# Turning x of two batches by DMA transposes instead of on TensorE, in an attention and mixture-of-experts kernel

## The chip, the core and the metric

The kernel runs on one core of a Trainium2 chip. The core has five engines with their own instruction streams: TensorE (PE, matmuls, with its weight loads shown apart as PEld), VectorE (DVE), ScalarE (ACT), GpSimd (POOL) and SyncE (SP), and 16 DMA engines that they share. SP does no arithmetic here: its stream issues most of the DMAs, one after the other, and POOL's issues the weight loads. The metric is the device time of one execution in microseconds (us); lower is better.

## The reference

q, k and v have the shape 8 batches, 8 heads, 576 positions, 64 wide. Sliding attention with a linear bias comes first, then a layer of 8 experts with dense weights P from 8 rounds of normalising rows and columns:

```python
scores = scale * np.matmul(q, k.transpose(0, 1, 3, 2))
mask = (rel >= 0) & (rel < 128)
scores = np.where(mask, scores + bias[None], -1000000000.0)
attn = softmax(scores)
x = (attn @ v).transpose(0, 2, 1, 3).reshape(4608, 512)
logits = x @ w_gate
P = np.exp(logits - logits.max())
for _ in range(8):
    P /= P.sum(1, keepdims=True) + 1e-09
    P /= P.sum(0, keepdims=True) + 1e-09
    P *= N / E
for e in range(8):
    out += P[:, e:e+1] * (np.maximum(x @ w1[e], 0.0) @ w2[e])   # w1: 512 x 1024, w2: 1024 x 512
```

## The kernel before

**Attention.** The loop over `steps` (line 694) goes through the batches b = 0 to 7; in each through five blocks of positions kb = 0 to 4 (four of 128 and a tail of 64); in each through two halves of the heads u = 0 and 1. A step is named (b, at) below, with at = 2 kb + u, so a batch has the steps (b, 0) to (b, 9). A step issues the next step's scores (L438) and their exponentials (L444, ACT) and masks (L449, DVE), then `values` (L472, PE), which DVE divides by its sums into `xsb` (L482, L483). After u = 1 of a block, `xsb` holds x for 128 positions, positions in the partitions.

**Turning x.** The experts and the gates need x with its columns in the partitions: the tile xT. `turn_x` does it for one block in one of two ways that `by_pe` chooses. On PE: four 128x128 matmuls against the identity into PSUM (L510) and a copy to xT on DVE (L521) or, in b 0, on ACT (L519). By transfer: one DMA transpose issued by SP from `xsb` to xT (L523). A turn on PE is issued in the first step of the block after (u = 0, behind that step's `values`); a turn by transfer at the end of the block's own second step. Before the change b 0, 1, 2 and 7 are turned on PE, b 3 to 6 by transfer (`XPE` is 3). Either way `keep_x` then issues a store of x to DRAM (L498), three blocks behind. The text writes turn 2.3 for block 3 of b 2. The tail's turn (2.4) goes to a tile of its own, shared by all the tails.

**Expert work between the steps.** Experts 0 and 1 are computed during the attention, in units of 4 blocks (one batch's x): eight groups of x @ w1 (L117, four matmuls each, a ReLU on ACT behind them, L129) and four of h @ w2 (L141, eight matmuls each, DVE copies the result, L559). `Filler` hands them out in the order (expert 0, batch n), (expert 1, batch n - 1). It counts an L117 group as 0.87 us and an L141 group as 1.74, and a step takes `budget` = backlog / `left` of it: a first piece of 1.0 ahead of `values`, the rest behind. A unit may start only when its blocks are below `filler.ready`. For b under 3 `ready` grows with the steps and reaches the batch's end, 4 b + 4, at the end of step (b, 8); for b above 3 it is set to 4 b at the end of step (b, 0), which lets in the batch before.

**SP's queue.** Its order is the program's order. In step (b, 1) stand a load of v (L391), stores of y (L545), `turn_qk` of the next batch (two DMA transposes of its q and k, L313) and the loads of a tail (L271); in (b, 3) a load of v and the 1 MB loads of q and k for batch b + 2 (L282); in (b, 5), (b, 7) and (b, 9) loads of v; in (b, 0) `turn_tail` (L337). The turns by transfer stand ahead of the load of v in the odd steps. q and k of a batch are cast to 16 bits in pieces by DVE (L298) and POOL (L296), from step (b - 2, 8) on; POOL also casts v (L404).

**Afterwards.** From step (6, 6) on POOL's queue loads weights of later experts. After the last step the last tail is turned, `gates` computes the logits of the eighth batch and the tails (L531), the normalising follows with expert work between its steps, and the experts 2 to 7 run over all of x (L992, L1029), read back from DRAM.

Of the kernel before, what the change touches and what calls it, by code (L numbers as in the profile page):

```python
# [14 lines left out]
def kernel(  # L15
# [15 lines left out]
    B, H, S, Dh = q.shape  # L31
# [36 lines left out]
    def x_of(blk):  # L68

        n = blk // 4  # L70
        if n not in xTs:
            tails = n == B
            xTs[n] = per.tile(
                [P, 4, NDT, P], FP16, name=f"xT_{n}", tag="xTt" if tails else "xT", bufs=1 if tails else 4
            )
        return xTs[n], blk % 4
# [94 lines left out]
    XPE, YO, XSB = 3, 7, 12  # L171
# [61 lines left out]
    if True:  # L233
# [179 lines left out]
        def sizes(kb):  # L413
            return P if kb < NKB - 1 else TL
# [38 lines left out]
        def values(b, kb, u):  # L453

            nk = sizes(kb)
            if u == 0:
                xsbs[b, kb] = asb.tile([P, H, Dh], FP16, name=f"xsb_{b}_{kb}", tag="xsb", bufs=XSB)
            psN = aps.tile([P, GT], FP32, name=f"psN_{b}_{kb}_{u}", tag="pmm", bufs=4)
            if b == 0:
                spin(psN, 3)  # L460
            psN = psN[:, 0 : 4 * Dh + 4].rearrange("p (h d) -> p h d", h=4)
            ops = []
            for y in range(2):
                for hb in range(2):
                    hh = 2 * y + hb
                    if kb > 0:
                        t, at = (pts[b, kb - 1, u], P) if kb < NKB - 1 else (pts[b, kb - 1, u], TL)
                        ops.append((hh, t[:, 2 * hb + y, at : at + P], vs[b, kb - 1][:, 4 * u + hh, 0 : Dh + 1]))
                    t, at = (pts[b, kb, u], P * (kb == NKB - 2)) if kb < NKB - 1 else (pts[b, kb - 1, u], 0)
                    ops.append((hh, t[:, 2 * hb + y, at : at + P], vs[b, kb][:, 4 * u + hh, 0 : Dh + 1]))  # L470
            for i, (hh, lhsT, rhs) in enumerate(ops):
                nc.tensor.matmul(  # L472
                    out=psN[:, hh, :],
                    lhsT=lhsT,
                    rhs=rhs,
                    start=(i == 0),
                    stop=(i == len(ops) - 1),
                )
            if kb > 0:
                pts.pop((b, kb - 1, u))  # L480
            rden = asb.tile([P, 4], FP32, name=f"rden_{b}_{kb}_{u}", tag="rden", bufs=2)
            nc.vector.reciprocal(out=rden[0:nk, :], in_=psN[0:nk, :, Dh])  # L482
            nc.vector.tensor_tensor(  # L483
                out=xsbs[b, kb][0:nk, 4 * u : 4 * u + 4, :],
                in0=psN[0:nk, :, 0:Dh],
                in1=rden[0:nk, :].unsqueeze(2).to_broadcast([nk, 4, Dh]),
                op=ALU.mult,
            )

        def by_pe(b):  # L490
            return b < XPE or b == B - 1

        kept: list = []

        def keep_x(left=0):
            while len(kept) > left:
                blk, lo, nk, xsb = kept.pop(0)
                nc.sync.dma_start(out=xd[blk, lo : lo + nk, :], in_=xsb[0:nk].rearrange("p h d -> p (h d)"))  # L498

        def turn_x(b, kb):  # L500
            nk = sizes(kb)
            blk = 4 * b + kb if kb < NKB - 1 else 4 * B + b // 2
            lo = 0 if kb < NKB - 1 else TL * (b % 2)
            xT, at = x_of(blk)
            to = xT[:, at, :, lo : lo + nk]
            xsb = xsbs.pop((b, kb))
            if by_pe(b):
                ps = aps.tile([P, NDT, P], FP16, name=f"psX_{b}_{kb}", tag="pmm", bufs=4)
                for j in range(NDT):
                    nc.tensor.matmul(  # L510
                        out=ps[:, j, 0:nk],
                        lhsT=xsb[0:nk, 2 * j : 2 * j + 2, :],
                        rhs=ident[0:nk, 0:nk],
                        is_transpose=True,
                        start=(j == 0),
                        stop=(j == NDT - 1),
                    )
                if b == 0:
                    nc.scalar.copy(out=to, in_=ps[:, :, 0:nk])  # L519
                else:  # L520
                    nc.vector.tensor_copy(out=to, in_=ps[:, :, 0:nk])  # L521
            else:
                nc.sync.dma_start(out=to, in_=xsb[0:nk].rearrange("p h d -> p (h d)"), transpose=True)  # L523
            kept.append((blk, lo, nk, xsb))
            keep_x(3)
# [141 lines left out]
        steps = [(b, kb, u) for b in range(B) for kb in range(NKB) for u in range(2)]  # L667
# [26 lines left out]
        for n, (b, kb, u) in enumerate(steps):  # L694
            nxt = steps[n + 1] if n + 1 < len(steps) else None
            at = 2 * kb + u
            left = ((10 - at) % 10 + 1) if b >= XPE else 10 - at + 9 * (at == 9)
            budget = filler.backlog() / (11 if (b, at) == (XPE, 0) else left)
            if b == 0:
                budget = 0.0  # L700
# [37 lines left out]
            if (b, kb, u) == (1, 1, 0):  # L738
                spin_alone(8)
            values(b, kb, u)  # L740
            if n > 0 and u == 0 and by_pe(steps[n - 1][0]):
                turn_x(*steps[n - 1][:2])
            if u == 1 and n // 2 + NKB < B * NKB:
                cast_v(n // 2 + NKB)
# [4 lines left out]
                filler.ready = 4 * b  # L749
            if at < 8 and b < XPE:  # L750
                filler.ready = 4 * b + at // 2
            if at == 8 and b < XPE:
                filler.ready = 4 * b + 4
            if u == 1 and not by_pe(b):
                turn_x(b, kb)
            if u == 1:
                if kb == 1 and b > 0:
# [62 lines left out]

        filler.fill(1.0)
        turn_x(B - 1, NKB - 1)
        keep_x()
        filler.fill(2.6)
# [433 lines left out]
```

## Time and profile before

| | |
|---|---|
| runs | 1004.63, 1005.24, 1005.81 us; median 1005.24 |
| profiled execution | 1004.29 us; span of its instructions 1002.5 us |
| TensorE clock granted | 1.000 of full speed |
| PE busy | 989.1 us (99%) |
| DVE, ACT, POOL busy | 762.1, 717.8, 104.7 us |
| chain that ended last | PE 91%, DMA 3%, DVE 3% |
| turns on PE: matmuls psX (L510) | 80, of them 64 of 128x128 and 16 of 64x64 |
| turns by transfer: xT<-xsb (L523) | 20, median 3.6 us from issue to landing |
| step times on PE | b 2: `values` of (2,1) at 80.67 us, of (3,0) at 105.36; b 7: `values` of (7,1) at 238.84, gates at 270.65 |

Attention and experts 0 and 1 fill about the first 330 us of the span; the rest belongs to the experts 2 to 7. In a timeline line the columns are the start, the duration, the engine, the line of the program, the operation with output and inputs, the count of instructions merged, and in brackets the idle time ahead of them with what ended it. In the chain of waits the columns are the start, the duration and what it was. For a DMA on SP the duration is the time that SP took to issue it, not the time to its landing.

### The profile page before, as it was taken

The numbers are of one execution on the slowest core, as the hardware profiler recorded it, in microseconds if no ns is written. First come the engines' busy times: TensorE is split into PE (matmuls) and PEld (weight loads), VectorE is DVE, ScalarE is ACT, GpSimd is POOL, SyncE is SP. The second block draws the span as 40 slices with busy tenths as digits, with TensorE's granted clock in tenths as the row PEclk, the third lists the DMA queues.
The fourth block names the chain that finished last, engine by engine and source line by source line (L and its number), as shares of the span: only waits on it lengthen the run. The fifth ranks groups of instructions, "written<-read, shape, count | busy, mean of one in ns | idle before, by whom it ended". The sixth has DMA issues, their size and how long they took to land.

```text
span 1002.5 us, 27939 instructions
## 1 busy us (share of the span) xinstructions
PE 989.1 (99%) x11591; PEld 801.5 (80%) x11591; DVE 762.1 (76%) x1598; ACT 717.8 (72%) x1216; POOL 104.7 (10%) x182
## 2 busy tenths in 40 slices
PE   7999999999999999999999999999999999999998
PEld 5645544445544899999999999999999999999997
DVE  6737676666688989887887887787787787787787
ACT  7654554555334768888888888888888888888885
POOL 3314344336010000000000000000000000000000
PEclk9999999999999999999999999999999999999999
DMA  9998788889998324324333334434433333433361
GB/s 250 212 261 226 158 217 225 216 182 191 237 187 170 75 50 99 79 61 98 80 64 96 80 70 86 85 68 84 87 82 66 96 75 67 99 75 65 96 117 48
DMA packets 264432, 122.46 MB, mean 122 GB/s; under 512 B 201969, under 2 KB 255729, under 8 KB 264305
## 3 DMA queue, kind: packets, MB, share of 16 engines
q1 hardware_dynamic: 249568, 102.68, 44.7%
q0 software_dynamic: 14304, 17.84, 10.6%
q8 instruction: 90, 1.47, 0.6%
q14 instruction: 38, 0.30, 0.1%
q10 hardware_dynamic: 432, 0.16, 0.1%
HBM read 78.30 MB, written 23.59 MB: 102 GB/s over the span
## 4 chain that ended last, share of the span: by engine, by line
PE 91%; DMA 3%; DVE 3%; ACT 1%; issue 0%; SPq 0%; POOL 0%; DVEq 0%
PE psM L1029 31%; PE psB L992 14%; PE psh L117 12%; PE psy L141 11%; PE psA L992 9%; PE psC L992 9%; DMA v<-in_v_dram 2%; PE psN L472 1%; PE psS L438 1%; DMA xT<-xsb 1%; PE psT L368 1%; DVE pt L449 0%; DMA q<-in_q_dram 0%; PE psG L531 0%; PE psh L971 0%
## 5 line engine op out<-in xcount | busy, mean ns | idle before, releaser
L1029 PEld LDWEIGHTS <-hs 128*128 128x128 f16 x2996 | 271.0, 98 | 22.4 <-DVE hs L1009 0.4
L1029 PE MATMUL psM<-w2l,hs 128*128 128x256 f16 x1440 | 186.6, 273 | 0.2 <-DVE hs L1009 0.2
L992 PEld LDWEIGHTS <-w1l 128*128 128x128 f16 x2848 | 181.4, 98 | 4.9 <-issue 0.5
L1005 ACT ACTIVATE hs<-hs 128x512 f16<-128x512 f16 x212 | 130.4, 630 | 35.3 <-DVE hs L1175 25.4
L1175 DVE TENSOR_TENSOR hs<-psB,s5y 128x512 f16<-128x512 f32 x106 | 73.3, 692 | 98.5 <-ACT xs L901 92.9
L992 PEld LDWEIGHTS <-s 128*128 128x128 f16 x2136 | 141.7, 98 | 6.4
L129 ACT ACTIVATE hT<-psh 128x512 f16<-128x512 f32 (+1 forms) x144 | 84.0, 586 | 78.9 <-PE psh L117 78.9
L117 PE MATMUL psh<-xT,w1t 128*128 128x512 f16 (+1 forms) x608 | 137.4, 368 | 2.5 <-DMA xT<-xsb 2.5
L901 ACT ACTIVATE xs<-xtok,L_sb 128x512 f16<-128x512 f16 x204 | 136.3, 721 | 1.8 <-DMA xset<-xs 1.8
L141 PE MATMUL psy<-w2t,hT 128*128 128x512 f16 x576 | 135.3, 379 | 0.0
L1029 PE MATMUL psM<-more,hs 128*128 128x256 f16 x864 | 129.5, 273 | 0.0
L992 PE MATMUL psA<-xset,w1l 128*128 128x128 f16 x1424 | 108.6, 219 | 0.0
L992 PE MATMUL psB<-xset,s 128*128 128x128 f16 x1424 | 108.6, 219 | 0.0
L444 ACT ACTIVATE pt<-psS 128x1024 f16<-128x1024 f32 x64 | 64.5, 1021 | 58.1 <-PE psS L438 57.6
L141 PEld LDWEIGHTS <-hT 128*128 128x128 f16 x576 | 53.5, 98 | 59.4 <-issue 1.7
L117 PEld LDWEIGHTS <-w1t 128*128 128x128 f16 x608 | 55.2, 98 | 55.4 <-issue 3.8
L1009 DVE TENSOR_TENSOR hs<-hs 128x1024 f16<-128x1024 f16 x107 | 73.9, 691 | 19.8 <-ACT hs L1005 17.7
L1166 ACT COPY psC<-psB 128x512 f32<-128x512 f32 x106 | 60.4, 570 | 38.8 <-PE psB L992 38.8
L449 DVE TENSOR_TENSOR pt<-pt,mask 128x1024 f16<-128x1024 f16 x64 | 49.2, 769 | 40.7 <-ACT pt L444 40.7
L559 DVE CAST yo<-psy 128x512 f16<-128x512 f32 x65 | 44.5, 689 | 44.7 <-PE psy L141 41.5
L1158 ACT COPY s5y<-psC 128x512 f32<-128x512 f32 x106 | 62.2, 587 | 22.7 <-PE psC L992 22.7
L1073 DVE TENSOR_TENSOR acc<-acc,psM 128x256 f32<-128x256 f32 (+1 forms) x162 | 73.9, 502 | 0.3
(127 smaller groups left out, 1421.0 us busy)
## 6 DMA issues: line engine op xcount, KB each, us to landing
s5y<-ysp SPq DMA_DIRECT2D x36, 256.0 KB, 3.0
ysp<-yo SPq DMA_DIRECT2D x65, 128.0 KB, 3.7
v<-in_v_dram SPq DMA_DIRECT2D x32, 256.0 KB, 4.7
out_dram<-acc SPq DMA_DIRECT2D x31, 256.0 KB, 2.5
q<-in_q_dram SPq DMA_DIRECT2D x5, 1024.0 KB, 6.5
k<-in_k_dram SPq DMA_DIRECT2D x5, 1024.0 KB, 8.8
xtok<-xd SPq DMA_DIRECT2D x34, 128.0 KB, 2.3
w2t<-in_moe_w_dram POOLq DMA_DIRECT2D x4, 1024.0 KB, 11.9
```

The costliest lines, as they stand in the source:

```text
L117: nc.tensor.matmul(out=ps[:, 0:nt], lhsT=w1ts[e][:, dt, P * ft : P * ft + P], rhs=xT[:, at : at + nb, dt, :], start=(dt == 0), stop=(dt == ...
L129: nc.scalar.activation(out=st["hT"][:, ft, 0:nt], in_=ps[:, 0:nt], func=AF.Relu)
L141: nc.tensor.matmul(out=ps, lhsT=st["hT"][:, ft, P * ms : P * ms + P], rhs=w2ts[e][:, ft, :], start=(ft == 0), stop=(ft == NFT - 1),)
L444: nc.scalar.activation(out=pt, in_=ps.rearrange("p a y n -> p (a y) n"), func=AF.Exp, scale=scale)
L901: nc.scalar.mul(out=xs[2 * (n % 2) + m], in_=xtok[m], mul=P_sb[:, blk, e : e + 1])
L992: nc.tensor.matmul(out=ps[:, j, :], lhsT=q[k][:, P * j : P * j + P], rhs=xset[n % 2][:, x, P * k : P * k + P], start=(start and j == 0 and ...
L1005: nc.scalar.activation(out=h[n][:, slot], in_=src, func=AF.Relu)
L1009: nc.vector.tensor_tensor(out=t[:, 4:6], in0=t[:, 0:2], in1=t[:, 2:4], op=ALU.add)
L1029: nc.tensor.matmul(out=Ms[bk][:, half, :], lhsT=h[n][:, LEFT[m], f, :], rhs=W2L[e][RIGHT[m]][:, f, :], start=(e == 2 and f == 0 and half = ...
L1073: nc.vector.tensor_tensor(out=a, in0=a, in1=p2, op=op)
L1158: nc.scalar.copy(out=s5, in_=pc)
L1175: nc.vector.tensor_tensor(out=h[n][:, 3], in0=pb, in1=s5, op=ALU.add)
```

## The change

`by_pe` takes the block as well as the batch: PE now turns b 0 and 1, and of b 7 only block 3 and the tail. So the five blocks of b 2 and the blocks 0 to 2 of b 7 are turned by transfer, at the end of their second step. For b 2, `ready` reaches 12 at the end of step (2,9) and not of (2,8), and in step (2,9) `left` is 1 and not 10; step (1,9) keeps its 10.

```diff
-        def by_pe(b):
-            return b < XPE or b == B - 1
+        def by_pe(b, kb):
+            return b < XPE - 1 or b == B - 1 and kb > 2
...
-            if by_pe(b):
+            if by_pe(b, kb):
                 ps = aps.tile([P, NDT, P], FP16, name=f"psX_{b}_{kb}", tag="pmm", bufs=4)
...
-            left = ((10 - at) % 10 + 1) if b >= XPE else 10 - at + 9 * (at == 9)
+            left = ((10 - at) % 10 + 1) if b >= XPE else 10 - at + 9 * ((b, at) == (1, 9))
...
-            if n > 0 and u == 0 and by_pe(steps[n - 1][0]):
+            if n > 0 and u == 0 and by_pe(*steps[n - 1][:2]):
                 turn_x(*steps[n - 1][:2])
...
-            if at == 8 and b < XPE:
+            if at == 8 + (b == XPE - 1) and b < XPE:
                 filler.ready = 4 * b + 4
-            if u == 1 and not by_pe(b):
+            if u == 1 and not by_pe(b, kb):
                 turn_x(b, kb)
```

## The prediction

> **What bounds the kernel now.** I read the page first, then the chain of waits, then the timelines of TensorE (PE) and of SP's queue around the third batch. On the page:
>
> ```profile
> PE 989.1 (99%) x11591; PEld 801.5 (80%) x11591; DVE 762.1 (76%) x1598; ACT 717.8 (72%) x1216; POOL 104.7 (10%) x182
> PE   7999999999999999999999999999999999999998
> DMA  9998788889998324324333334434433333433361
> xT<-xsb SPq DMA_TRANSPOSE x20, 3.6
> ```
>
> PE never rests after the first slices, so a microsecond taken off PE is a microsecond won, unless PE then waits. The first 13 slices (325 us, attention) also have the DMA engines nearly full, and the change puts more into them. The last line (DMA issues) is the kind that is added: 20 turns by transfer exist already, those of b 3 to 6, 3.6 us from issue to landing at the median (2.3 to 7.0). PE's list of waits holds such transfers twice (2.5 us in all), and the chain of waits shows both:
>
> ```profile
> 134.87 3.19 DMA xT<-xsb
> 198.50 6.50 DMA xT<-xsb
> ```
>
> They are turns 3.3 and 5.3 (batch.block): the first expert matmul over a batch's x stood 1.27 us at 138.10 and 1.23 at 205.13 until the fourth block had landed. The third batch pays no such wait today. PE there, at the hand-over to its expert work (start, duration):
>
> ```profile
> 97.72 0.41 PE L472 MATMUL psN<-v,pt 128*128 128x65 f16 x8
> 99.93 0.39 PE L510 MATMUL psX<-ident,xsb 128*128 128x128 f16 x4
> 102.53 0.41 PE L472 MATMUL psN<-v,pt 128*128 128x65 f16 x8
> 102.77 2.75 PE L117 MATMUL psh<-xT,w1t 128*128 128x512 f16 x12
> ```
>
> These are the values of step (2,7), which finish block 3; its turn on PE; the values of (2,9); and the first L117 over blocks 8 to 11, 5.05 us after the first line. SP's queue, first where b 2 has no turns, then b 4, which has them:
>
> ```profile
> 83.09 4.65 SPq L313 DMA_TRANSPOSE qk<-c  x2
> 90.53 0.71 SPq L282 DMA_DIRECT2D q<-in_q_dram  x1
> 91.28 1.69 SPq L282 DMA_DIRECT2D k<-in_k_dram  x1
> 93.01 2.68 SPq L498 DMA_DIRECT2D xd<-xsb  x1
> 96.21 3.03 SPq L498 DMA_DIRECT2D xd<-xsb  x1
> 99.98 0.61 SPq L391 DMA_DIRECT2D v<-in_v_dram  x1
> ```
>
> ```profile
> 144.88 1.21 SPq L523 DMA_TRANSPOSE xT<-xsb  x1
> 148.43 5.21 SPq L313 DMA_TRANSPOSE qk<-c  x2
> 158.72 0.63 SPq L282 DMA_DIRECT2D q<-in_q_dram  x1
> 162.56 1.65 SPq L523 DMA_TRANSPOSE xT<-xsb  x1
> 165.58 3.05 SPq L523 DMA_TRANSPOSE xT<-xsb  x1
> ```
>
> In both, SP issues without a gap: from 83.09 to past 99 in b 2 (the stores of x take 2.7 and 3.0 us to issue after the two 1 MB loads, against 0.6 elsewhere), and from 144.88 to 165.58 in b 4. SP serves in order, so a turn put there comes when its turn in the queue comes, not when its data is ready.
>
> **What leaves PE.** Eight turns, from the start of the turn to the next instruction on PE: 2.1 0.23 us (88.34 to 88.57), 2.2 0.22, 2.3 0.22 (0.32 less the 0.10 that any score matmuls cost behind another kind), 7.0 to 7.2 0.22 each. Turn 2.0 takes 0.98 from the end of the values ahead of it (81.66 + 0.24 = 81.90, to 82.88, with 0.28 of waiting for xsb). The tail 2.4 takes 0.31 (105.49 to 105.80). Together 2.6 us, of which 1.65 lies ahead of 102.77. Eight VectorE copies (L521, 0.41 us, the tail 0.28) go as well; VectorE is 6.6 us busy of 10 there, so they are worth nothing directly.
>
> **What the later letting-in moves.** Working the filler's costs through (L1_US, L2_US): before, ready becomes 12 after step (2,8), so (2,9) runs the last y matmuls, the values, then the first L117. After, ready becomes 12 at the end of (2,9), and (3,0) starts with that L117 ahead of its own values; left=1 only lets (2,9) finish its one remaining y piece. In PE's order the same pieces stand ahead of that L117. The wait is not shifted by half a block; what shifts is that the values of (3,0) to (3,2) come one or two L117 groups earlier, level again at (3,5). Nothing is added in work.
>
> **When PE asks for the third batch's x.** 102.77 - 1.65 = 101.1 us.
>
> **When it is there.** Turn 2.0 goes to SP behind the values of (2,1), whose xsb is done at 82.70, and SP is idle from 80.19. Behind it now stand one store of x, a load of v and two stores of y, then turn_qk: in b 4, 5 and 6 the head of turn_qk comes 3.55 us behind the first turn, so 86.25 instead of 83.09. From the first turn's issue to the landing of the fourth: b 3 27.4 us (110.63 to 138.06), b 4 26.0 (165.58 + 5.3), b 5 27.4, and b 6, which has no 1 MB loads, 23.6 (228.31 + 5.5). The queue of b 2 has one store of y fewer than b 4 (about 0.8 us). I take b 3 to 5, as b 2 has their loads: 82.7 + 26.5 - 0.8 = 108.4. The bounds are 104.0 (b 6's 18.1 us to the fourth issue and the shortest fourth landing, 3.2) and 110.1 (27.4 and no credit for the store).
>
> **The wait.** 108.4 - 101.1 = 7.3 us of idle PE, at a place where today is none; behind that L117 in PE's order are the values of (3,0) and all that follows. Net at that place 7.3 - 1.65 = +5.65; the tail turn takes it to +5.3. Also late, but under cover of this wait: the q and k of b 4, issued at about 97 instead of 90.5, land near 105 (q took 8.0), so VectorE stands at its cast of q (101.81 before) with the mask of (3,0) behind it, done by about 106. Should the turns come early, this is what is late next. The loads of v slip 5 to 6 us too; they are issued five blocks ahead. POOL's casts of b 4's k, in order between its casts of v, end later by as much, still ahead of b 3's turn_qk near 118.
>
> **Given back later.** With PE held, b 3's queue restarts level: its first turn about 115 (110.63 + the slip), its fourth landed 26.0 to 27.4 later, 141 to 142.3, where PE would ask at 108.4 + 33.75 = 142.15. So the 1.27 us of 138.10 should go: +4.0. I leave the 1.23 of b 5.
>
> **The eighth batch.** SP has idle time there, but the weight loads on POOL's queue fill the engines (share 1.08 to 1.20 from 240 to 272), and the nearest row, the tail's transpose at 239.59, took 10.6 us to land. Turn 7.2 can go at 255.3 (xsb of (7,5)); it lands by 266, and the gates read it at 270.65. Cost nothing with 4 us of cover; without it, up to 4. Three PE turns less: -0.66.
>
> **Sum.** +5.3 - 1.27 - 0.66 = +3.4 us. The profiled execution took 1004.29 us (span 1002.5), so 1007.7 in its terms; the median of the runs is 0.95 higher: 1005.24 + 3.4 = 1008.6.
>
> [...] The rows: four 128x128 turns take 0.22 us of PE against 3.6 us of landing. [...]
>
> **Rivals.** (1) *The queue keeps up, faster.* If the transfers spread, SP issues turn 2.3 soon after its xsb (about 98.0) and it lands within 3.2 us, by 101.2: no wait, and 1005.24 - 2.6 = 1002.6. It decides by whether turn 2.3 lands before 101.1. For it: 6.3, issued 1.1 us behind its values, and no wait in b 4 and 6. Against: SP had no gap until 99.3 even without turns. 0.14.
> (2) *A turn costs SP and the engines no more than a plain store of x* (0.58 us to issue, 3.2 to land, where b 4 has 1.21, 1.97 and 1.65): about 3.1 us less queue and 1.8 less landing, the x is there at 103.5, +0.75 at that place, and with the later terms (-0.31 - 1.27 - 0.66) 1003.7. Rows against it: xT's issues are 1.2 to 3.3 us. 0.08. [...]
> (3) *The eighth batch's gates wait as well*: turn 7.2 lands 2 to 4 us late, 1010.6 to 1012.6. 0.07.
> (4) *The lettings-in of b 4 to 6 shift*: b 4 has 0.1 us to spare (170.9 against 171.01) and b 5 stands 1.23; either sign, 0.05.
>
> **How the numbers follow.** The forecast has 0.66. Its own range, from landings at 104.0 to 110.1 and the 1.27 given back or not, is 1004.2 to 1011.6. A change under 0.2% (2.0 us) can't be told from none here. Faster: rival 1 and a little of 4, 0.15. Same: the low end of the forecast 0.11, rival 2 0.08, a little of 4, 0.20. Slower: 0.55 of the forecast, rival 3 and the rest, 0.65. The range, 1002.5 to 1011.6, reaches down to rival 1 and leaves out most of rival 3 and the far sides.
>
> **What would show it.** Right: in the profile after, the first L117 over blocks 8 to 11 waits 4 to 9 us for xT<-xsb near 101 to 109; SP issues turn 2.0 near 82.7, turn_qk near 86, q of b 4 near 97, turn 2.3 near 102 to 104; the wait at the next hand-over is shorter than 1.27; PE's busy time is lower by some 2 us with 32 fewer psX matmuls. Wrong: that wait is absent or under 2 us, or PE waits longest elsewhere (masks behind VectorE's cast, gates).

## The result and the profile after: 1.0% slower

The changed kernel takes 1015.46 us (median of five runs, 1011.56 to 1018.70) where the kernel before takes 1005.31 beside it (1004.63 to 1007.16): a ratio of 1.0098, with the interval 1.0079 to 1.0117, or +10.15 us. The prediction said 1008.6 and at most 1011.6: right in sign, far too small. The profiled execution took 1013.7 us with a span of 1011.9, 9.4 more than before; the working below is against that span. Of all the runs of this text one was slow, one of the eleven under "The clock alone" (1275.59 us at a clock of 0.753): it is in the median there and not in the ratio.

From the page after, busy time by engine and the granted clock of PE in 40 slices, and from the list of DMA issues the kind that was added:

```profile
PE 991.6 (98%) x11559; PEld 800.9 (79%) x11559; DVE 759.5 (75%) x1590; ACT 717.7 (71%) x1216; POOL 105.9 (10%) x182
PEclk9999899999999999999999999999999999999999
xT<-xsb SPq DMA_TRANSPOSE x28, 3.9
```

PE has 32 instructions fewer, as predicted, and yet 2.5 us more of busy time. The fifth slice of the clock (101 to 126 us) is an 8: there the clock was below full for a while. Before, every slice had a 9.

PE's list of waits, longest totals first (what waits, for what: us in all, times, longest):

```profile
PE psh L117 <- DMA xT<-xsb: 4.6, 1, 4.6
PE psG L531 <- DMA xT<-xsb: 2.2, 1, 2.2
...
PE psS L438 <- DVE qN L324: 1.9, 2, 1.2
...
PE psB L992 <- ACT psB L1154: 0.9, 1, 0.9
```

All four places are new. The 2.5 us over two waits, of before, have gone. The timeline of PE at the hand-over of the third batch:

```profile
108.86 1.87 PE L117 MATMUL psh<-xT,w1t 128*128 128x512 f16 x4 [4.63 <-DMA xT<-xsb]
...
110.75 3.40 PE L117 MATMUL psh<-xT,w1t 128*128 128x512 f16 x8
```

The first L117 over blocks 8 to 11 starts at 108.86, not 102.77. Then come the lines that no step of the prediction had: four L117 matmuls take 1.87 us and the next eight 3.40, while before twelve took 2.75. The same stretch by windows (length; busy us and instructions of PE, PEld, DVE, ACT, POOL; granted clock; DMA share; GB/s):

```profile
106.00:108.80 2.80, 0.00 (x0) 0.00 (x0) 0.57 (x1) 0.00 (x0) 0.71 (x2) 0.68 1.06 257
108.80:110.00 1.20, 1.14 (x3) 0.43 (x4) 0.00 (x0) 0.00 (x0) 1.09 (x3) 0.50 0.68 185
...
114.00:116.00 2.00, 2.00 (x19) 1.04 (x19) 0.27 (x1) 1.81 (x3) 1.42 (x3) 1.00 0.12 21
```

The mean of 0.68 over 106.0 to 108.8 is full speed to about 107.0 and half after it (0.99 over 106 to 107, 0.50 over 107 to 108): the clock fell about 2.8 us into the idle time, which began at 104.23 (108.86 less 4.63), and it was back at about 113.8 (0.50 over 112 to 113, 0.59 over 113 to 114, 1.00 over 114 to 116), 5 us after PE had work again. From 108.86 to 114.08 PE did in 5.22 us what takes about 2.77 at full clock (twelve L117 matmuls at 0.216 us, four of the values and the change to the scores): +2.45.

SP's queue ahead of that L117 (start, time to issue):

```profile
82.85 1.46 SPq L523 DMA_TRANSPOSE xT<-xsb  x1
...
86.67 4.88 SPq L313 DMA_TRANSPOSE qk<-c  x2
...
98.94 3.24 SPq L523 DMA_TRANSPOSE xT<-xsb  x1
...
105.46 1.21 SPq L523 DMA_TRANSPOSE xT<-xsb  x1
```

These are turn 2.0, turn_qk, turn 2.2 and turn 2.3. The load of q of b 4 is issued at 96.79. The chain is the one predicted, within 0.5 us up to that load, and turn 2.3 comes 1.5 us behind the far end of its 102 to 104. Two pieces of the chain of waits show the two landings that PE stood for, and two lines of the timeline the second stand, in the gates:

```profile
105.46 3.31 DMA xT<-xsb
...
260.28 17.57 DMA xT<-xsb
```

```profile
277.90 0.80 PE L531 MATMUL psG<-wg_sb,xT 128*128 128x8 f16 x24 [2.17 <-DMA xT<-xsb]
278.55 1.87 PE L117 MATMUL psh<-xT,w1t 128*128 128x512 f16 x4
```

Turn 7.2 took 17.6 us to land, not 10.6, and the L117 group behind the wait again ran at half speed (1.87 us for four).

The landmarks of the two profiled executions give the balance. First L117 over blocks 8 to 11: +6.09. Next hand-over (138.10 to 144.89): +6.79; 6.09 and the 2.45 of clock, less the tail turn's 0.31 and the 1.27 that was given back, make 6.96, within 0.2 of it. The hand-over of b 5 to b 6 (205.13 to 210.57): +5.44, as its 1.23 us of waiting were given back too. Gates (270.65 to 275.37): +4.72. From the gates to the first L856, 10.97 us instead of 7.59: +3.38, together +8.10, still the same at the first L992. Of the 3.38, 2.17 is the wait. The small matmuls of the gates were not slower for the clock (24 in 0.65 us, before 32 in 0.95); of the work behind them 2.51 us ran at half clock, which costs 1.25. Near the end it becomes +9.4.

### The profile page after: what moved, and what is told of

It is laid out like the page before. It is cut to its first block, busy times and chain, and to the rows that moved or that the text cites. A ratio compares the mean times of both kernels' runs of the same rounds, so it can differ in the third digit from the quotient of the medians.

```text
span 1011.9 us, 27879 instructions
## 1 busy us (share of the span) xinstructions
PE 991.6 (98%) x11559; PEld 800.9 (79%) x11559; DVE 759.5 (75%) x1590; ACT 717.7 (71%) x1216; POOL 105.9 (10%) x182
## 3 DMA queue, kind: packets, MB, share of 16 engines
q0 software_dynamic: 14304, 17.84, 10.6%
## 4 chain that ended last, share of the span: by engine, by line
PE 88%; DMA 7%; DVE 2%; ACT 1%; issue 1%; SPq 0%; POOL 0%; DVEq 0%; ACTq 0%; POOLq 0%
PE psM L1029 31%; PE psB L992 14%; PE psh L117 12%; PE psy L141 10%; PE psA L992 9%; PE psC L992 9%; DMA xT<-xsb 2%; DMA q<-in_q_dram 2%; PE psS L438 1%; PE psN L472 1%; DMA w2t<-in_moe_w_dram 1%; DMA xset<-xs 1%; PE psh L971 1%; DMA v<-in_v_dram 1%; ACT hs L1005 0%
## 5 line engine op out<-in xcount | busy, mean ns | idle before, releaser
L992 PEld LDWEIGHTS <-w1l 128*128 128x128 f16 x2848 | 181.4, 98 | 4.9 <-issue 0.5
L992 PEld LDWEIGHTS <-s 128*128 128x128 f16 x2136 | 141.6, 98 | 7.5 <-issue 1.0
L117 PE MATMUL psh<-xT,w1t 128*128 128x512 f16 (+1 forms) x608 | 141.0, 375 | 4.6 <-DMA xT<-xsb 4.6
L992 PE MATMUL psB<-xset,s 128*128 128x128 f16 x1424 | 108.5, 219 | 0.9 <-ACT psB L1154 0.9
L992 PE MATMUL psA<-xset,w1l 128*128 128x128 f16 x1424 | 108.6, 219 | 0.0
L117 PEld LDWEIGHTS <-w1t 128*128 128x128 f16 x608 | 55.7, 99 | 59.1 <-issue 5.7
```

The lines of the kernel that those rows point to most:

```text
L117: nc.tensor.matmul(out=ps[:, 0:nt], lhsT=w1ts[e][:, dt, P * ft : P * ft + P], rhs=xT[:, at : at + nb, dt, :], start=(dt == 0), stop=(dt == ...
L992: nc.tensor.matmul(out=ps[:, j, :], lhsT=q[k][:, P * j : P * j + P], rhs=xset[n % 2][:, x, P * k : P * k + P], start=(start and j == 0 and ...
```

## The experiments

Each kernel ran beside the kernel before on the same chip (its medians there: 1003.78 us for the first four, 1004.65 for the next four, 1004.75 for the last four). A figure such as +7.4 is the difference of two medians. "Theory" is that the two stands and the clock behind them make the loss.

**The third batch alone.** Batch 7 stays on PE.

```diff
-            return b < XPE - 1 or b == B - 1 and kb > 2
+            return b < XPE - 1 or b == B - 1
```

> Only the third batch is turned by transfer; all of the eighth goes back to TensorE. Theory (two places, each with a wait and a slow clock behind it): the first L117 over blocks 8 to 11 still waits 4 to 7 us near 104 to 109, the clock falls to about half for some 5 us behind it, the gates do not wait, and the time is 5 to 8 us over the kernel before, about 3.5 less than the changed kernel. Rival (all of the loss comes from the third batch, the gates are late only because of it): the same time as the changed kernel, some 10 us over the kernel before.

1011.22 us, ratio 1.0078 (1.0060 to 1.0096), +7.4. In its timeline of PE:

```profile
108.01 1.87 PE L117 MATMUL psh<-xT,w1t 128*128 128x512 f16 x4 [4.32 <-DMA xT<-xsb]
```

The stand and the half clock are there, the gates (274.60) wait for no transfer, and the first L856 stands 7.59 us behind them as before. So the third batch carries most of the loss, but not all.

**The eighth batch's three blocks alone**, with the letting-in of before.

```diff
-            return b < XPE - 1 or b == B - 1 and kb > 2
+            return b < XPE or b == B - 1 and kb > 2
...
-            left = ((10 - at) % 10 + 1) if b >= XPE else 10 - at + 9 * ((b, at) == (1, 9))
+            left = ((10 - at) % 10 + 1) if b >= XPE else 10 - at + 9 * (at == 9)
...
-            if at == 8 + (b == XPE - 1) and b < XPE:
+            if at == 8 and b < XPE:
```

> Only the blocks 0 to 2 of the eighth batch are turned by transfer; the third batch and its letting-in are as before. Theory: no wait near 103; turn 7.2 takes 13 to 18 us to land among the weight loads, the gates wait 2 to 5 us and the clock is down behind them: 2 to 5 us over the kernel before. Rival (the eighth's transfers are late only because the third batch pushed everything back): no wait at the gates, 0.5 to 0.7 us under the kernel before.

1009.05 us, ratio 1.0060 (1.0038 to 1.0082), +5.3. Turn 7.2, issued at 255.62, landed 18.7 us later; the gates in the timeline:

```profile
274.33 0.76 PE L531 MATMUL psG<-wg_sb,xT 128*128 128x8 f16 x24 [3.13 <-DMA xT<-xsb]
```

The L117 group behind them takes 1.86 us, half speed again. This part costs 5.3 us with the third batch on PE, so a step costed at nothing was the second error. The two parts add up to 12.7, more than the whole change; in the profiled spans it is 5.3 and 6.4 against 9.4. Some 1.4 of this comes near the end of the span in each of the three kernels, and so counts twice in the sum (it is taken up again below). And from the gates to the first L856 this kernel loses 4.75 us, the changed kernel, whose gates come later and stand shorter (2.17 against 3.13 us), 3.38. The rest goes the other way: the half clock at the hand-over lasts twice as long in the changed kernel as with the third batch alone.

**TensorE kept busy ahead of both places.** `spin_alone(n)` issues n matmuls into a spare PSUM tile.

```diff
+            if (b, at) == (XPE, 0):
+                spin_alone(44)
             got = filler.fill(1.0) if b else 0.0
...
+        spin_alone(22)
         gates(4 * B - 4, NBLK)
```

> The changed kernel with TensorE kept busy where it would stand: 44 idle-work matmuls of 256 columns (some 4.7 us) ahead of the first L117 over blocks 8 to 11, and 22 (some 2.4 us) ahead of the gates. They do nothing for the result. Theory (the idle time costs again by the clock that falls behind it): the granted clock stays at 1.00 through 105 to 116 and 276 to 284, the matmuls behind take 0.22 us each instead of 0.43, and the time is 3 to 4 us under the changed kernel. Rival (the slow matmuls come from the transfers that still run, not from the idle time): slow as before, no gain or a loss of up to 2 us.

1012.75 us, ratio 1.0089 (1.0076 to 1.0102), +9.0: a miss, about 1 us gained of the 3 to 4 expected. The timeline says where the rest went:

```profile
101.78 3.29 PE L141 MATMUL psy<-w2t,hT 128*128 128x512 f16 x8
...
110.23 1.03 PE L117 MATMUL psh<-xT,w1t 128*128 128x512 f16 x4
```

Behind the spins the L117 groups run at full speed (1.03 us for four). But the clock had already fallen, to 0.52 over 102 to 105, behind two score waits of 1.03 and 0.64 us close together, so that a y piece took 3.29 us instead of 1.90; and the 44 spins (105.32 to 110.23) overran the landing by about 1.4 us. Behind the 22 spins the gates still waited 0.97 us, at full clock (1.02 us for the four L117 matmuls behind them). Like pairs of score waits in the changed kernel (1.24 and 0.63) and in the one with the third batch alone (1.03 and 0.64) did not lower the clock: it is 1.00 over 102 to 104 in both. The clock was seen, its price was not isolated: the second spin experiment, below, mends this.

**The third batch let in as b 3 to 6 are**, that is inside b 3 (`XPE - 1` for `XPE` in `left`, `budget` and `ready`), batch 7 on PE.

> Third batch by transfer, the eighth on TensorE, and the third batch's expert work let in as that of the batches 3 to 6 is: at the end of step (3,0), with the work before it spread over eleven steps. Now three L141 pieces and three values stand between the values of (2,7) and the first L117 over blocks 8 to 11 (some 9 us), where the changed kernel has two of each. Theory (the wait is the landing of turn 2.3 less what PE has ahead of it): the wait shrinks from 4.6 to 1 to 3 us, little or no time at half clock, 1 us under to 2 over the kernel before. Rival (SP's queue moves back with the stores of y, so that the landing slips with the letting-in): the wait stays 4 to 5 us, 5 to 8 over the kernel before.

1009.43 us, ratio 1.0056 (1.0044 to 1.0068), +5.6: the time lies in the rival's range, and the wait between the two. The L117 still stands 3.46 us, until 108.29. PE spent the time that it had won in another wait, in this line of its timeline:

```profile
103.99 0.30 PE L472 MATMUL psN<-v,pt 128*128 128x65 f16 x4 [1.15 <-DVE pt L449]
```

That is the mask behind VectorE's cast of q, which the prediction had named as late next.

**Queue order, in two steps.** First all of it: turn_qk of b 3 issued ahead of turn 2.0, and the 1 MB loads of b 4's q and k moved from step (2,3) to (2,7), with their casts; batch 7 on PE.

```diff
-            if u == 1 and not by_pe(b, kb):
+            if u == 1 and not by_pe(b, kb) and (b, at) != (XPE - 1, 1):
                 turn_x(b, kb)
...
                     turn_qk(b + 1)
+                    if b == XPE - 1:
+                        turn_x(b, kb)
...
-            if 1 <= b < B - 2 and at == 3:
+            if 1 <= b < B - 2 and at == (7 if b == XPE - 1 else 3):
```

> Third batch by transfer, eighth on TensorE. In SP's queue turn_qk of batch 3 goes ahead of turn 2.0, and the 1 MB loads of q and k of batch 4 go from step (2,3) to (2,7), behind turn 2.3, with their first casts moved from (2,8) and (2,9) to (3,0). Theory (turn 2.3 is late because of what stands ahead of it on SP and on the DMA engines): it is issued near 97 to 100 and lands by 102 to 104, the first L117 over blocks 8 to 11 waits 0 to 2 us, the clock stays at 1.00, and the time is within 2 us of the kernel before. Rival (the transfers are slow of themselves, or something else sets the landing): landing near 108 and 5 to 8 us over the kernel before.

1009.12 us, ratio 1.0043 (1.0026 to 1.0059), +4.5: a miss. The stand at this place did go, as the theory said, with turn 2.3 issued at 100.32 and landed 2.6 us later, and the L117 at 103.56 at full speed (1.02 us for four). It came back one batch on; a line of VectorE's timeline and one of PE's:

```profile
108.78 1.10 DVE L298 CAST c<-q 128x512 f16<-128x512 f32 x3 [2.88 <-DMA q<-in_q_dram]
...
141.41 1.05 PE L117 MATMUL psh<-xT,w1t 128*128 128x512 f16 x4 [3.59 <-DMA xT<-xsb]
```

The late load of q holds VectorE for a while. But what PE waits for now is turn 3.3, and SP issues it no later than in the next kernel (137.97 against 138.15): PE comes earlier and stands for it, and behind the stand PE is slow again: from 142.27 on, four matmuls of the values and twelve of L117 take 4.39 us, and 2.72 in the kernel before (138.97 to 141.69), so by estimate 3.3 us of it ran at half clock. This profiled execution was also 1.9 us late from its start (the first L117 of all at 26.21, before at 24.31). Then only the first two edits, without the loads moved:

> Third batch by transfer, eighth on TensorE; of the changes to SP's order only that turn_qk of batch 3 stands ahead of turn 2.0. Theory: the copies of k on POOL run near 90 to 95 again, before those of q on VectorE near 96, so these take 0.55 us each and not 1.4, and TensorE's wait of 1.7 us in the scores of (3,0) goes; but the chain up to turn 2.3 is as long as before, it lands near 108 all the same, and the wait there grows by what the scores no longer wait: 5 to 7 us, time as with the third batch alone (within 2 us of it). Rival (the late q and k are what costs): 2 us or more under the third batch alone.

1010.44 us, ratio 1.0062 (1.0045 to 1.0078), +5.8. The score waits are gone, and the L117 stands 4.24 us, to 106.05, at half clock behind it (0.69, 0.50, 0.96 in the three windows of 2 us from 106). The stand didn't grow as expected, because turn 2.3 was issued 2.0 us earlier too (102.63, with the third batch alone 104.62), and the L117 started 2.0 earlier (106.05 against 108.01). In both kernels it starts with the landing: the landing sets the end. What the score waits cost by themselves this run doesn't show.

**The weight loads written behind the gates** in the program, in the kernel with the eighth batch alone.

> Eighth batch's blocks 0 to 2 by transfer, third on TensorE, and the 1 MB weight loads of the experts 4 to 6 issued behind the gates and not ahead of them. Theory (turn 7.2 is late because it shares the DMA engines with the weight loads): it lands in 6 to 11 us and not 17, the gates wait 0 to 1 us, clock 1.00, time within 1.5 us of the kernel before. Rival (the transfer is slow for another reason): landing 15 us or more, wait 2 to 4, some 5 us over the kernel before.

1009.68 us, ratio 1.0051 (1.0032 to 1.0069), with turn 7.2 landing 18.3 us after its issue. This tests neither side: nothing in POOL's stream waits for the gates, and it issued the same 1 MB loads at 253.63 and 255.28, still ahead of turn 7.2 (256.17). The gates waited 2.87 us, and here the clock stayed at 1.00 through 270 to 284. It fell elsewhere (0.97 over 100 to 150), behind the one wait for turn 3.3 (1.95 us, to 139.10), at a place that the edit doesn't touch; a line of PE's timeline there:

```profile
140.16 4.38 PE L117 MATMUL psh<-xT,w1t 128*128 128x512 f16 x12
```

**Only blocks 0 and 1 of the eighth batch by transfer** (`kb > 1` in the edit of the eighth batch alone).

> Eighth batch's blocks 0 and 1 by transfer, block 2 back on TensorE, third batch on TensorE. Theory (only the last of the three is needed too early): turn 7.1 still takes 13 to 17 us but has 18 to 20 us until the gates, no wait there, time 0.4 us under to 1 us over the kernel before. Rival (three or two, the transfers hold up the stores and the casts behind them): still 3 to 5 us over.

1004.38 us, ratio 1.0001 (0.9988 to 1.0014). No transfer is waited for at the gates. All of the +5.3 hangs on the one block that is needed soonest after its issue.

**The 1 MB loads held back** until turn 7.2 has landed, by a POOL instruction that reads its result; the rest as in the kernel with the eighth batch alone.

```diff
+        nc.gpsimd.tensor_copy(out=mx_sb[:, 3:4], in_=x_of(4 * B - 2)[0][:, 2, 0, 0:1])
         load_last(4)
         load_last(E - 3)
```

> Eighth batch's blocks 0 to 2 by transfer, third on TensorE, and POOL's queue really held: a one-column copy on POOL that reads the result of turn 7.2 stands ahead of the 1 MB weight loads of the experts 4 to 6, so these cannot be issued before turn 7.2 has landed (moving them in the program alone, as in the run before this, left them where they were, since POOL waits for nothing there). The 256 KB loads stay. Theory (turn 7.2 shares the engines with the weight loads): it lands in 9 to 13 us, not 17, the gates wait 0 to 1 us, the time is within 1.5 us of the kernel before. Rival (the landing is long without the 1 MB loads too): 15 us or more, a wait of 2 to 4 us, some 5 us over the kernel before.

1004.93 us, ratio 1.0007 (0.9996 to 1.0019). POOL's timeline:

```profile
265.71 0.19 POOL L815 CAST mx_sb<-xT 128x1 f32<-128x1 f16 x1 [14.78 <-DMA xT<-xsb]
```

The 1 MB loads follow at 266.17 and 266.92. Turn 7.2, issued at 254.99, landed 10.6 us later, the figure that the prediction had taken from a transpose ahead of these loads, and the gates (270.08) wait for nothing. So the two 1 MB weight loads issued ahead of it make up the other 8 us.

**The clock alone.** The kernel with turn_qk first, and 34 spins at (3,0).

> Third batch by transfer with turn_qk ahead of turn 2.0, eighth on TensorE, and 34 idle-work matmuls (3.6 us, less than the wait of 4.2 there, so that they add nothing) in the place where TensorE waits for turn 2.3. Theory (the clock falls because of the idle time and costs on top of it): clock 1.00 behind the wait, the first L117 groups at 0.22 us a matmul, 1.5 to 2.5 us under the same kernel without them, so 3 to 4.5 us over the kernel before. Rival (the clock falls from the load or costs nothing): as without them, 5.5 to 6.5 us over the kernel before.

1007.67 us, ratio 1.0029 (1.0016 to 1.0043), +2.9 against +5.8 without the spins. The timeline of PE:

```profile
107.02 1.02 PE L117 MATMUL psh<-xT,w1t 128*128 128x512 f16 x4 [1.04 <-DMA ysp<-yo]
...
108.01 1.89 PE L117 MATMUL psh<-xT,w1t 128*128 128x512 f16 x8
```

The spins fill 102.11 to 105.98, and the idle time left is 1.04 us (put down to a store of y; turn 2.3 was issued at 103.50). The L117 starts 0.97 us later than without the spins, and still the second piece of values behind it starts 0.69 earlier (111.25 against 111.94). The stand ends no sooner, but its tail at half clock, 1.66 us, is gone: that is the term missing from the prediction, by itself. Not all of it is left later: this execution was some 0.5 us late ahead of this place (turn_qk at 83.38 against 82.90), turn 2.3 landed later, and the next hand-over waits 0.44 us for turn 3.3, so that the gates stand 0.48 earlier (272.33 against 272.81). The other 1.3 of the 1.8 us between the profiled spans (1006.2 and 1004.4) comes near the end, where this kernel lacks a wait of 0.87. The two ratios differ by 0.33%, about 3.3 us; what they show beyond the spans was not traced.

**Idle time alone.** The kernel before, with PE made to wait once at the head of (3,0) for a chain of copies on ACT; not one transfer more.

```diff
+            if (b, at) == (XPE, 0):
+                pause(14)    # one matmul that reads a tile which ACT writes 14 times
             got = filler.fill(1.0) if b else 0.0
```

> The kernel before with nothing turned differently, and TensorE made to stand once at the head of step (3,0): one matmul there reads a scratch tile that ScalarE writes in 14 copies in a row (14 x 0.37 us), all of it idle-work. The cost of idle time by itself, without any added transfer. Theory: TensorE is idle about 5 us, the clock is down to half from about 3 us into it until some 5 us behind it, and the time is 6 to 8 us over the kernel before: the idle time and about 2.4 us more (less up to 1.3 us if the wait at the next hand-over goes). Rival (idle time costs itself): 3.5 to 5 us over.

1013.73 us, ratio 1.0091 (1.0076 to 1.0106), +9.0. The pause was longer than planned, 7.02 us, and not all of the +9.0 is the pause (below). Timeline and windows:

```profile
114.65 0.40 PE L275 MATMUL psJ_q<-pause_z 128*128 128x256 f16 x1 [7.02 <-ACT pause_z L273]
114.84 1.91 PE L117 MATMUL psh<-xT,w1t 128*128 128x512 f16 x4
```

```profile
110.00:112.00 2.00, 0.00 (x0) 0.00 (x0) 0.14 (x1) 1.84 (x6) 1.41 (x3) 0.79 0.00 0
...
116.00:118.00 2.00, 2.00 (x12) 0.93 (x11) 0.95 (x4) 0.60 (x1) 0.00 (x0) 0.51 0.00 0
118.00:120.00 2.00, 2.00 (x16) 0.84 (x15) 0.18 (x1) 1.08 (x2) 0.00 (x0) 1.00 0.00 0
```

The clock falls about 3.5 us into the idle time (0.79 over 110 to 112 is full speed to about 111.15), with no transfer at work from 110, and is back at 118.0, over 3 us after PE resumes. So idle PE alone lowered the clock, to 0.50 over 112 to 116, without one added transfer. The wait of the next hand-over fell from 1.27 to 0.47 us, and that of b 5 to b 6 is gone: a pause here is given back in part later on, as the prediction had it.

In the profiled execution PE was late before the pause: the first L117 of all starts at 27.47 (before 24.31), and the values of (2,7) still stand 2.86 behind (100.58). At the gates it is 9.58, so 6.72 arose in between. The pause of 7.02 and half of the 3.33 us of work behind it that ran at half clock, less the 0.80 and 1.23 given back, make 6.66. Idle time alone would have made 5.0. The mean clock of this execution, 0.995 over 1012.0 us, is some 10 us at half by estimate, and 6.84 of them are the stretch at the pause; where the rest lies is not shown.

Read by windows of 1 us or less, the stretches at half clock have one length in five places, whatever the idle time was: 3.42, 3.42, 3.41 and 3.42 us (the third batch alone at 107.82, the eighth alone at 274.98, turn_qk first at 106.75, the first spins at 102.12) and 3.40 at the gates of the changed kernel (277.66); and in three twice that, 6.84: at the changed kernel's hand-over (106.98), with the later letting-in (106.46) and here (111.14). In two more, with the loads of q and k moved and with the weight loads written later, they are some 3.3 us by estimate, from the 4.39 us that the same sixteen matmuls take behind the stand in both (from 142.27 and from 139.98) and the 2.72 at full clock. Where windows show it, they begin between 1.6 us (the later letting-in) and 4.9 us (turn_qk first) after PE went idle (with the first spins 2.5 after the first of two waits began), in three kernels 0.6 to 0.7 us after it had work again (the eighth alone, turn_qk first, the first spins). The cost is half of the PE work that falls into the stretch, the small matmuls of the gates apart: at the changed kernel's hand-over 4.96 us of it, so 2.48, where 2.45 was measured.

How much idle time it takes is not one figure in these runs: 2.17 us was enough at the gates of the changed kernel, and in the kernel with the weight loads written later 1.95 was enough at one place and 2.87 was not at another. What decides it was not shown.

**Transfers only where their reader is far off.** Block 3 of every batch, block 2 of b 2 and b 7 and the tail of b 7 on PE, the rest of b 2 to 7 by transfer; turn_qk first; the letting-in of before.

```diff
-            return b < XPE - 1 or b == B - 1 and kb > 2
+            return b < XPE - 1 or kb == 3 or b in (XPE - 1, B - 1) and kb == 2 or b == B - 1 and kb == 4
```

> Each batch from the third on keeps on TensorE the turns that are needed soon, and only those: block 3 of the batches 2 to 6, blocks 2 and 3 of the third, blocks 2 and 3 and the tail of the eighth; the rest by transfer, with turn_qk of batch 3 ahead of turn 2.0. Letting-in as in the kernel before. Theory (a turn by transfer costs nothing where 10 us or more lie between it and its reader): no wait for xT<-xsb over 0.5 us at any hand-over (two of 1.2 to 1.3 us in the kernel before), 1 to 3.5 us under the kernel before. Rival (added transfers always push other loads back): a new wait of 1 us or more on v, q or k, same time or slower.

1002.15 us, ratio 0.9976 (0.9965 to 0.9987), 2.4 us under the kernel before by the ratio. PE at the third batch's hand-over:

```profile
103.40 2.75 PE L117 MATMUL psh<-xT,w1t 128*128 128x512 f16 x12
```

No instruction of PE waits for a transfer of x at any place, so the waits of 1.27 and 1.23 us are gone too, and the clock is 1.000. Turn 7.1 took 17.0 us to land here, but the gates read it 23.8 us after its issue. Which of its edits brings how much was not taken apart.

## Why the prediction was wrong, point by point

- *When the x is there*: right. 108.77 against 108.4; turn_qk at 86.67 against 86.25, q of b 4 at 96.79 against 97, turn 2.3 at 105.46 against 102 to 104. Its place and its size by landing (+6.09 against +5.65 at that L117) are right too. PE would have asked at 102.4 and not 101.1 (108.86 less its waits of 4.63, 1.24 and 0.63); as the landing sets the end, that cost nothing.
- *The wait, 7.3 us of idle PE*: the step that failed first. It priced the idle time at its own length. The half clock behind it cost 2.45 us more, in no bound of the range. All of the working ran on rows of a trace with the clock at 1.000, and the longest wait in PE's list there was 1.3 us, so no row showed this price; the pause and the spins show it.
- *What is late next*: the direction was right, the instruction not the first. POOL's copies of b 3's k began at 94.97 instead of 90.03 and ran beside VectorE's of q, so that scores waited 1.24 and 0.63 us. By the rows this came out of the same stand and cost nothing (SP issued without a gap up to turn 2.3, so PE's waits didn't hold it); no run isolates it. That VectorE is 6.6 us busy of 10 holds for 102 to 112; over 80 to 105, where most of its copies went, it was 19.9 of 25.
- *Given back later*: right for the 1.27 (+6.79 at that hand-over would have been +8.06). The 1.23 that I left was given back as well, which is rival 4 on its good side.
- *The eighth batch, cost nothing with 4 us of cover*: the second step that failed. 10.6 us of landing was read from a tail's transpose at 239.59, ahead of the 1 MB loads; turn 7.2 is issued behind them and took 17.6. Rival 3 was this case, at a chance of 0.07, and it too priced the wait alone: 2.17 us of waiting became +3.38.
- *Three PE turns less, the tail*: the three turns are right (from +5.45 at the first L117 over the seventh batch, 237.96 to 243.41, to +4.72 at the gates: -0.73 against -0.66); the tail's -0.31 is too small to be seen among the other terms of its hand-over.
- *Rivals 1 and 2*, a queue that keeps up and a turn as cheap as a store: refuted by SP's rows, 1.2 to 3.2 us for each of the four turns against 0.58 for most stores of the same bytes.

The sum with the measured terms: 6.09 + 2.45 - 0.31 - 1.27 - 1.23 - 0.66 = 5.07 at the gates (4.72 measured), + 3.38 there = 8.10 with the measured figure, and 1.3 more near the end. Of that last part 0.87 us is the wait at 987.53 in PE's list above; behind it ACT stood 2.34 us for a read of x from DRAM (xset<-xs). The kernel before and four of the experiments' (both with spins, the one with the pause and the last) do not have this wait, the others have 0.3 to 0.9 us of it; nothing was run on it, and its cause is open. So is the 0.7 us by which the runs' median exceeds what the profiled execution shows.

## What to carry to other kernels

Price a stall of TensorE as the idle time and, from some 2 us on (here 1.95 us brought it, 1.57 did not), one or two stretches of 3.4 us at half clock, of which the part that reaches into the work behind counts half. It is a price to expect and not a sure one: a stall of 2.87 us had none, nor, by estimate, had one of 2.4 us for v in the first 60 us of the kernel with the loads of q and k moved (its mean clock of 0.998 over 1007.8 us is 3 to 5 us at half, and 3.3 of them lie behind 142.27). In these runs a transfer took work off PE for nothing only where its reader came later than the slowest landing among the same neighbours in the queues (8.0 us in the batches 2 to 6 of the changed kernel, 18.7 behind weight loads in the kernel with the eighth batch alone); keep the block that is needed soonest on the engine, as the last experiment does. Read a landing from a row with the same loads ahead of it, not from the nearest in time.

## What the runs showed of the hardware that was not expected

- Half clock, in stretches of 3.4 or 6.8 us: a 128x512 matmul takes 0.43 us in them (from 111.17 to 112.87 in the changed kernel) instead of 0.216. Single waits of 1.23 and 1.27 us (the kernel before) and 1.57 (the 1 MB loads held back) did not bring it, the one of 1.95 did. Two waits close together stood ahead of it once: 1.03 and 0.64 us, in one kernel of three with such a pair.
- One turn of 128 KB landed in 2.4 to 8.0 us in the batches 2 to 6 of the changed kernel, and over the kernels in 10.6 to 18.7 for the blocks 0 to 2 of the eighth, beside the weight loads of POOL's queue. For block 2, moving the loads in the program changed little (18.7 and 18.3); making POOL wait took it to 10.6.
- VectorE's 128x512 copies of b 3's q took 0.60 us each before, behind POOL's like copies of k, and 1.20 at the median (0.92 to 1.49) where these ran at the same time; with turn_qk first and the loads of q and k moved, two of them take 1.11 us once more, as before. Two lines of their groups (count, shortest, median and longest ns), both from the changed kernel.

```profile
L324 POOL COPY kN<-qk x4: 1062/1258/1471, 95.0 to 98.4; 128x512 f16<-128x512 f16 x4
L324 DVE COPY qN<-qk x4: 923/1204/1491, 96.1 to 100.8; 128x512 f16<-128x512 f16 x4
```
